# Sparse attention and FFN on one core: first loads reordered, and weight loads tied to the conversion of earlier ones

## The chip, the core and the metric

The kernel runs on one NeuronCore of a Trainium2 chip. The metric is device microseconds of one execution; three runs of the kernel before gave 869.53, 871.46 and 873.02, median 871.46. The engines are TensorE (PE, its weight loads shown as PEld), VectorE (DVE), ScalarE (ACT), GpSimd (POOL) and SyncE (SP), which issues nearly all DMA transfers. Each engine works through its own instructions strictly in the order written.

## The reference

```python
# q, k, v: (8, 8, 576, 64); heads 0-3 local mask, heads 4-7 strided mask, stride 32
scores = where(mask[h], q @ k.T / sqrt(64), -1e9)
attn = softmax(scores);  x = (attn @ v) laid out as (8 * 576, 512)
h = x @ w_in                          # (512, 2048)
out = (h * clip(h + 3, 0, 6) / 6) @ w_out     # (2048, 512)
```

`w_in` and `w_out` arrive as 64-bit floats; each is 8 MB.

## The kernel before

The eight batches are done one after another. For batch 0 attention runs first: four pairs of heads, g = 0 to 3, in the order local, strided, local, strided. For each pair q and k are loaded and turned upright by matmuls with an identity (L372), scores go to PSUM (L609, L601), the softmax runs over DVE, ACT and POOL (L634 to L666), the probabilities are transposed (L685 on DVE for strided pairs, L372 and L721 for local ones), and the product with v is made (L389 for the first local pairs, L736 for strided ones). Two copies (L427 on ACT, L430 on DVE) then make one quarter of x, as a high and a low part. The four quarters x are in the order of the pairs; the products ph (L857 to L859) of the FFN add over all four, so the FFN of batch 0 runs freely only once the fourth quarter is there. Until the first ph there are filler matmuls (L1571, "idle") wherever the plan sees PE unused.

A weight block k (0 to 31; here `parts[k]`, four blocks of w_in, four of w_out, and so on) is 128 x 512 doubles, 512 KB, loaded by one DMA (L274) into `raw`. It is turned into a high and a low single-precision part: `high` (ACT, L282), `low` (ACT, L286), `join` (DVE, L290), `hi` (ACT L304 or POOL L306), `lo` (POOL, L309). Blocks 0 to 7 serve the first four columns of the FFN of batch 0, blocks 8 to 15 the next four.

The order of every engine comes from a planner, `Plan.emit`: each `op` has an engine, an estimated duration, a due time and the keys it reads and writes; the planner simulates, always starting the operation that can start first and, among those, the one that is due first. `early` is the earliest start, `after` the time a load takes in the planner's model of DMA, `room` an extra margin behind an input. What is written out is a fixed order; on the chip the engines keep it, whatever the real times are.

SP issues in this order at the start: q and k of batch 0 (k of g = 0, 1 from ACT), v of g = 0 (L378, L381: rows of 256 bytes), v of g = 1 (L567: 2 KB), weight blocks 0 to 3, v of g = 2 (256 bytes again), v of g = 3, weight blocks 4 to 15, then q, k and v of batch 1 (L358, L567, L362, L367), among which the later weight blocks come.

Of the kernel before, what the change touches and what calls it, by code (L numbers as in the profile page):

```python
# [12 lines left out]
I32 = mybir.dt.int32  # L13
# [6 lines left out]
P = 128  # L20
# [9 lines left out]
TOK = 512  # L30
TURNS = ((0, 2, 1, 3), (2, 0, 3, 1)) + ((0, 2, 1, 3),) * 6
AHEAD = 27.0
OPEN = 6.0
HIENG = {"ACT": 0.63, "POOL": 0.7}

# [25 lines left out]
class Plan:  # L61
# [12 lines left out]
    def op(self, engine, us, fn, reads=(), writes=(), due=0.0, room=0.0, mode="", after=0.0, take=None, give=None, early=0.0):  # L74
        n = len(self.ops)
        before = set()
        for k in reads:
            if k in self.wrote:
                before.add(self.wrote[k])
            self.used.setdefault(k, []).append(n)  # L80
        for k in writes:
            if k in self.wrote:
                before.add(self.wrote[k])
            before.update(self.used.pop(k, ()))
            self.wrote[k] = n
        before.discard(n)
        how = engine if isinstance(engine, dict) else {engine: us}
        self.ops.append((how, fn, before, due, room, mode, after, take, give, early))
        return n
# [85 lines left out]
def attention_ffn(ctx: ExitStack, tc, q, k, v, w_in, w_out, out):  # L175
    nc = tc.nc
# [9 lines left out]
    NQ = 4  # L186
# [3 lines left out]
    wp = ctx.enter_context(tc.tile_pool(name="wp", bufs=1))  # L190
# [7 lines left out]
    op = plan.op  # L198
    tiles = {}

    def new(pool, key, shape, dtype, name):

        tag = "_".join(str(x) for x in key)
        t = tiles[key] = pool.tile(shape, dtype, tag=tag, name=name)
        return t
# [52 lines left out]
    def wkey(w, g, i):  # L258
        return ("w", w, g, i)

    def weight_part(k, w, g, i):
        key = wkey(w, g, i)
        fc = FQ * g if w == "i" else FQ * g + i + 1
        due = T0 + fc * TILE / NFC - 5.0 + 0.01 * k
        fkey = ("x", 1, 1 - (k // 2 % 2 if k < 20 else 0), k % 2)
        name = f"{w}{g}{i}"

        def load():
            if w == "i":
                src = w_in[i * P:(i + 1) * P, g * TOK:(g + 1) * TOK]  # L270
            else:
                src = w_out[(g * FQ + i) * P:(g * FQ + i + 1) * P, :]
            raw = new(wp, key, [P, TOK, 2], I32, f"raw{name}")
            nc.sync.dma_start(raw, src.bitcast(I32).rearrange("p (n t) -> p n t", t=2))  # L274

        def bits():
            raw = tiles[key]
            return raw.rearrange("p n t -> p (n t)")[:, :TOK]

        def high():  # L280
            f = new(xp, fkey, [P, TOK], I32, f"f{name}")
            nc.scalar.activation(f.bitcast(F32), tiles[key][:, :, 1].bitcast(F32), AF.Prelu, scale=2.0 ** -112, alpha=2.0 ** 32)  # L282

        def low():
            raw = tiles[key].bitcast(U16).rearrange("p n (t u) -> p n t u", u=2)[:, :, 0, 1]
            nc.scalar.activation(bits(), raw, AF.Copy, scale=2.0 ** -13, bias=2.0 ** -14 - 0.5)  # L286

        def join():
            f = tiles[fkey]
            nc.vector.scalar_tensor_tensor(out=f, in0=f, scalar=3, in1=bits(),  # L290
                                           op0=ALU.logical_shift_left, op1=ALU.bitwise_or)

        def whole():
            f = tiles[fkey].bitcast(F32)
            return f if w == "i" else f.rearrange("p (h e d) -> p h d e", h=2, d=2)

        def part(x):
            t = tiles[key][:, x]
            return t if w == "i" else t.rearrange("p (h d e) -> p h d e", h=2, d=2)

        def hi(e):
            new(wp, key, [P, 2, TOK], F32R, f"w{name}")
            if e == "ACT":
                nc.scalar.copy(part(0), whole())  # L304
            else:
                nc.gpsimd.tensor_copy(part(0), whole())  # L306

        def lo():
            nc.gpsimd.tensor_tensor(out=part(1), in0=whole(), in1=part(0).bitcast(F32), op=ALU.subtract)  # L309

        op("SP", 0.53, load, writes=[key], due=-49 + 0.01 * k if k < 4 else -48.4 + 0.01 * k if k < 6 else -2 + 0.1 * k if k < 16 else due - 20.0, early=7.0 if k < 16 else due - 30.0, after=1.6 if k < 16 else 1.25)
        op("ACT", 0.68, high, reads=[key], writes=[fkey], due=due - 5, room=LATE + 1.0)
        op("ACT", 0.68, low, writes=[key], due=due - 5)
        op("DVE", 1.05, join, reads=[key], writes=[fkey], due=due - 3)
        op(HIENG, 0, hi, reads=[fkey], writes=[key], due=due - 2)
        op("POOL", 1.3, lo, reads=[fkey, key], writes=[key + ("lo",), key], due=due - 1)


    nn = [0]
# [24 lines left out]
    def timing(g):  # L344
        b = g // NPAIR
        if not b:
            return T0 - 6.0 * (NPAIR - g)
        return wanted[b] - 6.0 - (NPAIR - 1 - g % NPAIR) * (wanted[b] - opens[b]) / NPAIR
# [92 lines left out]
    def pair(g):  # L441
# [3 lines left out]
        loc = h0 < H // 2  # L445
        nm = f"{b}_{c}"
        early = (b == 0) + (g == 0)
        due = timing(g)
# [30 lines left out]
        for x in "qk":  # L479
# [6 lines left out]
            if early:  # L486
# [32 lines left out]
                for h in range(2):  # L519
                    op({"ACT": 0.45, "DVE": 0.4} if loc else {"ACT": 0.65, "DVE": 0.65}, 0, partial(evac, h=h), reads=[tb[h]],  # L520
                       writes=[tkey[x]] if h == 0 else [(tkey[x], 1)], give=tb[h], due=due - 19)
# [13 lines left out]
            op("SP", 3.4 if b > 4 else 2.8, load, writes=[nkey], due=due - 35, early=due - 45, after=2.0)  # L535
            op("DVE", 0.8 if loc else 1.25, tr, reads=[nkey, "plain"], writes=[tkey[x]], due=due - 18, early=max(due - AHEAD, T0 + OPEN), room=LATE)


        first = b == 0 and loc
        vkeys = [("vt",) if loc else ("vs",)]  # L540
        if first:
            vkeys = [wkey("i", NQ - 1, j) if c else ("n", j) for j in range(2)]
# [6 lines left out]
        elif b == 0:  # L549
            vkeys = [wkey("i", NQ - 1, c)]  # L550
# [7 lines left out]
        def load_v():  # L558
# [6 lines left out]
            rows = v[b, h0:h0 + 2].rearrange("j (m a t) d -> a m j (t d)", a=4, t=8)  # L565
            for a in range(4):
                nc.sync.dma_start(tiles[vkey][PAD * a:PAD * a + NPOS].rearrange("p j t d -> p j (t d)"), rows[a])  # L567
        op("SP", 2.6 if first else 1.6 if loc else 2.1, load_v, writes=vkeys, due=(-52, -48.8, -48.7, -48.5)[g] if early else due - 30, early=0 if early else due - 35, after=3.2 if first else 2.0)


        ekeys = [("el" if loc else "es", j) for j in range(2)]
# [4 lines left out]
        w = 2 * PAD if loc else NPOS  # L576
# [37 lines left out]
        for j in range(2):  # L614
# [5 lines left out]
            def keep(j=j):  # L620
# [17 lines left out]
               writes=[ek, st], give=banks[j], due=sd + 0.5)  # L638
# [874 lines left out]
            second_of(s)  # L1513
    nk, no, nz = [0], [0], [0]

    parts = [(w, g, i) for g in range(NQ) for w in "io" for i in range(4)]

    def first_tiles():
        tiles["qplain"] = ap.tile([P, S + STRIDE * PAD], F32, tag="qq", name="qplain")
# [14 lines left out]
    for g in range(NPAIR):  # L1534
        pair(g)
# [4 lines left out]
    for n, part in enumerate(parts):  # L1540
        weight_part(n, *part)
# [3 lines left out]
    for g in range(NPAIR, 4 * NPAIR):  # L1545
        pair(g)
    keep_plain()
    ffn(1)
    for g in range(4 * NPAIR, 5 * NPAIR):
        pair(g)  # L1550
# [54 lines left out]
```

## Time and profile before

| | us |
|---|---|
| median of three runs | 871.46 |
| lowest and highest | 869.53, 873.02 |
| the profiled execution, its own time | 870.54 |
| its span in the profile | 868.8 |

The profile is of one execution, with a mean granted TensorE clock of 0.991. Times in it are microseconds from the start of the span, 1.7 us of the execution lie outside it. A row of the timeline merges like instructions: start, busy time, engine, line, operation, tiles, shape, count, and in brackets the idle time of the engine before it with what ended it. "issue" there means that the engine waited for nothing that the profile shows.

### The profile page before, as it was taken

Reading aid. Unit: us, or ns where it says so; the run is one execution under the profiler, and the core shown is the slowest. Engines: PE = TensorE matmul, PEld = TensorE weight load, DVE = VectorE, ACT = ScalarE, POOL = GpSimd, SP = SyncE. Lnnn points to the kernel's source line nnn. Section 1 sums busy time; section 2 is a strip of 40 time slices with the busy share of each in tenths; the row PEclk is TensorE's granted clock in tenths of the full one; section 3 lists DMA queues with packets and bytes.
Section 4 is the critical chain, followed back from the end, with each engine's and each line's share of the span. In section 5 each row is a group of like instructions: output and inputs, shape, how many; then the busy total and the mean of one; then the engine's idle time right before and its main releaser. Section 6 shows DMA issues by size and latency. Waiting matters only on the chain.

```text
span 868.8 us, 18930 instructions
## 1 busy us (share of the span) xinstructions
PE 846.6 (97%) x6954; PEld 683.0 (79%) x6954; DVE 537.6 (62%) x898; ACT 557.9 (64%) x1246; POOL 615.3 (71%) x606
## 2 busy tenths in 40 slices
PE   8899999999999999999999999999999999999996
PEld 7577778788888788888888888788888778888884
DVE  6588878344454538454546664566767888555586
ACT  4587657678778866877677955776744645454441
POOL 5488876687547799767676994465974987767573
PEclk9899999999999999999999999999999999999998
DMA  8978713798974455899999898876566667866536
GB/s 199 313 158 240 231 30 83 205 290 237 295 216 116 119 129 159 219 268 250 243 285 287 272 314 212 230 206 197 180 203 188 190 179 223 243 195 194 182 122 145
DMA packets 323308, 179.12 MB, mean 206 GB/s; under 512 B 182864, under 2 KB 300368, under 8 KB 323216
## 3 DMA queue, kind: packets, MB, share of 16 engines
q1 hardware_dynamic: 318564, 176.27, 71.8%
q10 hardware_dynamic: 4652, 1.64, 0.9%
q8 instruction: 55, 0.90, 0.4%
q14 instruction: 37, 0.30, 0.1%
HBM read 136.97 MB, written 40.89 MB: 205 GB/s over the span
## 4 chain that ended last, share of the span: by engine, by line
PE 87%; POOL 5%; DVE 4%; ACT 2%; issue 2%; POOLq 0%; DVEq 0%; ACTq 0%
PE P L1130 8%; PE P L1131 8%; PE P L1132 8%; PE cP L1453 5%; PE cP L1454 5%; PE cP L1455 5%; PE acc L834 5%; PE ph L857 5%; PE ph L858 4%; PE ph L859 4%; PE acc L835 4%; PE acc L836 4%; PE acc L1215 4%; PE acc L1217 3%; PE acc L1216 3%; PE pv L736 2%
## 5 line engine op out<-in xcount | busy, mean ns | idle before, releaser
L1471 DVE SCALAR_TENSOR_TENSOR C<-cP,C 128x512 f32<-128x512 f32 x96 | 65.7, 687 | 40.5 <-PE cP L1455 39.8
L795 POOL TENSOR_TENSOR gl<-u,gh 128x512 fp32r<-128x512 f32 x48 | 65.2, 1360 | 34.1 <-ACT gh L791 17.9
L1142 DVE TENSOR_TENSOR G<-P,G 128x512 f32<-128x512 f32 x64 | 44.0, 689 | 65.1 <-PE P L1132 52.7
L1130 PE MATMUL P<-B_T,wr 128*128 128x512 f32 x192 | 76.1, 397 | 3.9 <-ACT G L1137 2.3
L834 PE MATMUL acc<-wo,gh 128*128 128x512 f32 x192 | 77.3, 403 | 0.0
L836 PE MATMUL acc<-wo,gl 128*128 128x512 f32 x192 | 75.2, 392 | 0.3 <-POOL gl L795 0.2
L835 PE MATMUL acc<-wo,gh 128*128 128x512 f32 x192 | 75.1, 391 | 0.0
L1131 PE MATMUL P<-B_T,wr 128*128 128x512 f32 x192 | 74.9, 390 | 0.0
L1132 PE MATMUL P<-B_T,wr 128*128 128x512 f32 x192 | 74.9, 390 | 0.0
L1137 ACT COPY G<-P 128x512 f32<-128x512 f32 x64 | 37.5, 586 | 52.3 <-PE P L1132 51.9
L1368 POOL TENSOR_TENSOR sp<-G,sp 128x512 fp32r<-128x512 f32 x34 | 47.5, 1408 | 24.8 <-ACT sp L1364 22.6
L666 POOL TENSOR_TENSOR e<-e,st 128x144 f32<-128x144 f32 (+1 forms) x64 | 44.2, 693 | 18.8 <-DVE st L662 15.7
L780 DVE SCALAR_TENSOR_TENSOR u<-u,ph 128x512 f32<-128x512 f32 x48 | 32.8, 684 | 38.2 <-ACT u L777 38.1
L857 PE MATMUL ph<-x,wi 128*128 128x512 f32 x128 | 52.6, 411 | 2.3 <-ACT x L427 1.2
L701 ACT COPY atloc<-e 32x192 f32<-32x192 f32 x144 | 50.8, 353 | 2.5 <-DVE e L691 1.1
L858 PE MATMUL ph<-x,wi 128*128 128x512 f32 x128 | 51.0, 398 | 0.6 <-DVE x L430 0.5
L859 PE MATMUL ph<-x,wi 128*128 128x512 f32 x128 | 50.8, 397 | 0.0
L777 ACT ACTIVATE u<-ph,three 128x512 f32<-128x512 f32 x48 | 33.0, 687 | 27.2 <-PE ph L859 26.9
L1130 PE MATMUL P<-B_B,wr 128*128 128x512 f32 x120 | 47.1, 393 | 0.0
L1131 PE MATMUL P<-B_B,wr 128*128 128x512 f32 x120 | 46.8, 390 | 0.0
L1130 PEld LDWEIGHTS P<-B_T,wr 128*128 128x128 f32 x192 | 36.1, 188 | 13.7 <-ACT G L1137 3.6
L1132 PE MATMUL P<-B_B,wr 128*128 128x512 f32 x120 | 46.8, 390 | 0.0
(604 smaller groups left out, 2648.1 us busy)
## 6 DMA issues: line engine op xcount, KB each, us to landing
wr<-dA SPq DMA_DIRECT2D x72, 256.0 KB
or<-do SPq DMA_DIRECT2D x32, 512.0 KB
wr<-dSu SPq DMA_DIRECT2D x48, 256.0 KB
wr<-dSv SPq DMA_DIRECT2D x48, 256.0 KB
or<-do SPq DMA_DIRECT2D x48, 256.0 KB
rawi<-in_moe_w_in_dram SPq DMA_DIRECT2D x16, 512.0 KB
rawo<-in_moe_w_out_dram SPq DMA_DIRECT2D x16, 512.0 KB
do<-wo SPq DMA_DIRECT2D x16, 512.0 KB
```

The costliest lines, as they stand in the source:

```text
L701: nc.scalar.copy(at[PAD * (a + h):PAD * (a + h) + PAD, :, rows], e[rows, :, PAD * h:PAD * h + PAD])
L795: (nc.vector if tail else nc.gpsimd).tensor_tensor(out=to, in0=src(), in1=tiles[gk[0]].bitcast(F32), op=ALU.subtract)
L834: nc.tensor.matmul(acc, gh, woh, start=fc == 0, stop=False)
L835: nc.tensor.matmul(acc, gh, wol, start=False, stop=False)
L836: nc.tensor.matmul(acc, gl, woh, start=False, stop=end)
L857: nc.tensor.matmul(ph, wih, xh, start=n_ == 0, stop=False)
L858: nc.tensor.matmul(ph, wih, xl, start=False, stop=False)
L859: nc.tensor.matmul(ph, wil, xh, start=False, stop=n_ == NCC - 1)
L1130: nc.tensor.matmul(ph, wh, xh, start=fresh and k == 0, stop=False, skip_group_check=not fresh)
L1131: nc.tensor.matmul(ph, wh, xl, start=False, stop=False, skip_group_check=not fresh)
L1132: nc.tensor.matmul(ph, wl, xh, start=False, stop=k == 1, skip_group_check=not fresh)
L1471: nc.vector.scalar_tensor_tensor(out=tiles[ck], in0=tiles[bank], scalar=1.0 / 6.0, in1=tiles[ck], op0=ALU.mult, op1=ALU.add)
```

## The change

Three things change. The due times of the first loads are altered so that SP's order becomes: v of g = 0, v of g = 1, weight blocks 0 and 1, v of g = 2, weight blocks 2 and 3, v of g = 3, block 4. After `lo` of block k, for k from 0 to 10, POOL writes one element pair into the tile `raw` of block k + 5; that tile is made then. The load of block k + 5 writes the same tile, so for blocks 5 to 15 SP waits for that write, and the planner knows the load to depend on `lo` of the block five ahead. Sizes, arithmetic and the blocks from 16 on are as before.

```diff
+PACE = 5
...
+    parts = [(w, g, i) for g in range(NQ) for w in "io" for i in range(4)]
+    raws = {}
+
+    def raw_of(k):
+        if k not in raws:
+            raws[k] = new(wp, wkey(*parts[k]), [P, TOK, 2], I32, "raw{}{}{}".format(*parts[k]))
+        return raws[k]
+
     def weight_part(k, w, g, i):
         key = wkey(w, g, i)
+        paced = PACE <= k < 16
...
-            raw = new(wp, key, [P, TOK, 2], I32, f"raw{name}")
+            raw = raw_of(k)
...
         def lo():
             nc.gpsimd.tensor_tensor(out=part(1), in0=whole(), in1=part(0).bitcast(F32), op=ALU.subtract)
-
-        op("SP", 0.53, load, writes=[key], due=-49 + 0.01 * k if k < 4 else -48.4 + 0.01 * k if k < 6 else -2 + 0.1 * k if k < 16 else due - 20.0, early=7.0 if k < 16 else due - 30.0, after=1.6 if k < 16 else 1.25)
+            if k + PACE < 16:
+                nc.gpsimd.memset(raw_of(k + PACE)[:1, :1], 0)
+
+        op("SP", 0.53, load, reads=[("paced", k)] if paced else [], writes=[key], due=(-49, -48.99, -48.8, -48.79)[k] if k < 4 else -48.4 + 0.01 * k if k < 6 else -2 + 0.1 * k if k < 16 else due - 20.0, early=7.0 if k < 16 else due - 30.0, after=1.6 if k < 16 else 1.25)
...
-        op("POOL", 1.3, lo, reads=[fkey, key], writes=[key + ("lo",), key], due=due - 1)
+        op("POOL", 1.3, lo, reads=[fkey, key], writes=[key + ("lo",), key] + [("paced", k + PACE)] * (k + PACE < 16), due=due - 1)
...
-        op("SP", 2.6 if first else 1.6 if loc else 2.1, load_v, writes=vkeys, due=(-52, -48.8, -48.7, -48.5)[g] if early else due - 30, early=0 if early else due - 35, after=3.2 if first else 2.0)
+        op("SP", 2.6 if first else 1.6 if loc else 2.1, load_v, writes=vkeys, due=(-52, -49.5, -48.9, -48.7)[g] if early else due - 30, early=0 if early else due - 35, after=3.2 if first else 2.0)
```

## Rows read from the trace of the kernel before

**Rows 1.** From the page: busy time of each engine with its instructions, and the DMA queue that carries code.

```profile
PE 846.6 (97%) x6954; PEld 683.0 (79%) x6954; DVE 537.6 (62%) x898; ACT 557.9 (64%) x1246; POOL 615.3 (71%) x606
q8 instruction: 55, 0.90, 0.4%
```

**Rows 2.** Stretches of the span: start and end, length, busy time and instruction count of each engine, granted clock, DMA share, GB/s.

```profile
0.00:23.62 23.62, 21.45 (x602) 16.94 (x603) 15.74 (x42) 11.31 (x26) 11.28 (x34) 1.00 0.84 208
...
20.00:30.00 10.00, 4.95 (x162) 4.07 (x160) 6.83 (x21) 4.29 (x10) 2.94 (x6) 0.86 0.81 224
30.00:40.00 10.00, 10.00 (x125) 6.43 (x124) 5.43 (x13) 6.68 (x20) 6.81 (x10) 0.80 0.97 358
40.00:50.00 10.00, 9.93 (x135) 7.45 (x135) 7.37 (x18) 8.90 (x20) 6.70 (x9) 1.00 1.07 322
50.00:60.00 10.00, 8.32 (x41) 6.19 (x38) 7.50 (x11) 8.36 (x17) 9.25 (x8) 0.83 0.50 94
60.00:70.00 10.00, 9.93 (x166) 7.83 (x165) 8.07 (x16) 8.05 (x16) 9.84 (x10) 1.00 0.87 224
145.00:243.00 98.00, 98.00 (x979) 78.79 (x979) 45.71 (x96) 76.08 (x211) 63.44 (x78) 1.00 0.84 244
```

**Rows 3.** The timeline of PE, 20 to 39 us.

```profile
22.73 0.89 PE L389 MATMUL pv<-at,v 64*64 64x32 f32 x44
27.93 1.07 PE L389 MATMUL pv<-at,v 64*64 64x32 f32 x28 [4.31 <-issue]
28.93 4.21 PE L1571 MATMUL idle<-ident 128*128 128x384 f32 x6
33.07 1.63 PE L736 MATMUL pv<-atstr,v 128*64 128x72 f32 x32
34.62 1.14 PE L601 MATMUL ps<-kt,qt 64*64 64x36 f32 x64
35.69 2.20 PE L1571 MATMUL idle<-ident 128*128 128x384 f32 x6
38.69 0.50 PE L857 MATMUL ph<-x,wi 128*128 128x512 f32 x1
```

**Rows 4.** DMA packets of three stretches: 17.9 to 21.0, 21.0 to 25.2, and 25.2 to 25.4 with the code queue in it. A weight row is one packet of 4 KB, so the packets under 8 KB less those under 2 KB are weights.

```profile
DMA packets 217, 0.82 MB, mean 266 GB/s; under 512 B 16, under 2 KB 16, under 8 KB 217
...
DMA packets 822, 1.26 MB, mean 299 GB/s; under 512 B 545, under 2 KB 545, under 8 KB 822
...
DMA packets 153, 0.07 MB, mean 327 GB/s; under 512 B 149, under 2 KB 149, under 8 KB 152
...
q8 instruction: 1, 0.02, 41.5%
```

**Rows 5.** The same view of 13 to 16 us, when v of g = 0 is coming in.

```profile
DMA packets 1566, 0.46 MB, mean 154 GB/s; under 512 B 1523, under 2 KB 1523, under 8 KB 1566
```

**Rows 6.** The timeline of SP's queue: start and length of the issue of each group of loads.

```profile
16.40 2.79 SPq L274 DMA_DIRECT2D rawi<-in_moe_w_in_dram  x4
19.23 0.66 SPq L378 DMA_DIRECT2D v<-in_v_dram  x1
23.25 1.86 SPq L381 DMA_DIRECT2D v<-in_v_dram  x2
29.15 2.37 SPq L274 DMA_DIRECT2D rawo<-in_moe_w_out_dram  x4
34.41 4.01 SPq L274 DMA_DIRECT2D rawo<-in_moe_w_out_dram  x4
39.46 7.65 SPq L358 DMA_DIRECT2D qn<-in_q_dram  x4
59.39 1.95 SPq L358 DMA_DIRECT2D qn<-in_q_dram  x4
61.44 2.07 SPq L358 DMA_DIRECT2D kn<-in_k_dram  x4
63.55 2.73 SPq L274 DMA_DIRECT2D rawi<-in_moe_w_in_dram  x4
```

**Rows 7.** Timelines of DVE, ACT and POOL, 25 to 38 us.

```profile
25.59 1.75 DVE L685 STREAM_TRANSPOSE atstr<-e 32x256 f32<-32x256 f32 x4
29.29 0.46 DVE L430 TENSOR_TENSOR x<-pv,x 128x288 fp32r<-128x288 f32 x1 [1.95 <-ACT x L427]
30.87 0.82 POOL L649 TENSOR_TENSOR e<-e,st 96x384 f32<-96x384 f32 x1 [4.86 <-DVE st L645]
33.55 1.28 POOL L309 TENSOR_TENSOR wi<-fi,wi 128x512 fp32r<-128x512 f32 x1
37.01 0.55 POOL L641 TENSOR_TENSOR e<-e,mtri 128x144 f32<-128x144 f32 x1 [2.18 <-ACT e L627]
```

**Rows 8.** Timelines of DVE and PE, 48 to 58 us.

```profile
48.90 2.37 DVE L290 SCALAR_TENSOR_TENSOR fo<-fo,rawo 128x512 int32<-128x512 int32 x3
51.20 0.61 DVE L430 TENSOR_TENSOR x<-pv,x 128x256 fp32r<-128x256 f32 x1
51.78 1.20 DVE L290 SCALAR_TENSOR_TENSOR fi<-fi,rawi 128x512 int32<-128x512 int32 x1
49.27 1.22 PE L736 MATMUL pv<-atstr,v 128*64 128x72 f32 x32
53.57 0.50 PE L858 MATMUL ph<-x,wi 128*128 128x512 f32 x1 [0.48 <-DVE x L430]
```

**Rows 9.** The shortest memset of POOL, from the timeline of the first microseconds.

```profile
0.24 0.10 POOL L1589 MEMSET const-float32-0.0<- 128x1 f32 x1 [0.24 <-issue]
```

**Rows 10.** Timelines of POOL and PE, 55 to 67 us: `lo` of weight block 8, and the first product of the second group of columns, which reads it.

```profile
55.98 1.28 POOL L309 TENSOR_TENSOR wi<-fi,wi 128x512 fp32r<-128x512 f32 x1
66.05 0.39 PE L857 MATMUL ph<-x,wi 128*128 128x512 f32 x1
```

## What the change is expected to do

> **What bounds the kernel now.** I read the page first: PE is busy 846.6 us of the 868.8 [rows 1]. In the stretches PE is full from 60 us on, at full clock, with DVE and POOL well below it in the bulk; what it lacks lies before 60 us: 5 of 10 us busy in 20 to 30, and a clock of 0.86, 0.80 and 0.83 in three of the four stretches after 20 [rows 2]. So the change, which acts before 70 us, is worth what it moves the moment from which the FFN runs freely. That is 53.57, when the fourth quarter of x arrives [rows 8].
>
> The next view is PE's timeline there [rows 3]. In the middle of one product, after 44 of 72 like instructions, PE stops for 4.31 us, from 23.62 to 27.93, and the trace names nothing that it waits for. All its inputs are there: the same tiles serve the instructions before and after. I read this as a wait for code. The code queue moved 55 blocks in the whole run, 0.90 MB, so 16 KB each, and PE has 2 x 6954 = 13908 instructions [rows 1], 253 to a block; none of the other engines has near as many. PE had run 602 + 603 of them when it stopped [rows 2]. One block starts between 25.2 and 25.4 [rows 4], 2.6 us before PE goes on.
>
> Why so late? The four weight loads were issued from 16.40 to 19.2 [rows 6]. Their 4 x 128 rows are 512 packets of 4 KB; 201 ran from 17.9 to 21.0, 277 from 21.0 to 25.2, and only 3 in the stretch in which the code block starts [rows 4]. The block began just when the weights had drained. Its request must have come before the stop, since 1205 instructions had then been run and the pieces of code come one by one; about 21 us is my estimate.
>
> [...]
>
> **The change, part by part.**
>
> *Order of v and weights.* Blocks 0 and 1, then v of g = 2, then blocks 2 and 3. Nothing changes up to block 1, so PE reaches the stop at 23.62 as before. Of 256 weight packets, 201 are gone by 21.0 [rows 4]; at 277 in 4.2 us, 66 a us, the rest takes 0.8, until 21.8. Behind them come the 256-byte rows of v: 2 x 64 x (8 + 9) + 64 = 2240. Those of g = 0 ran at 1523 in 3 us, 508 a us [rows 5], so they take 4.4 us. If the code block has to wait only for the weights it starts at 21.8, and PE resumes 2.6 later, at 24.4, which is 3.5 earlier. If it waits for all of v as well it starts at 26.2: no gain. SP needed from 19.23 to 25.1 to hand out these v loads [rows 6], so at 21.8 about a third is not yet in the queue, and I take a start at 22.8 and a return at 25.4: 2.5 earlier, bounds 0 and 3.5.
>
> [...]
>
> *The clock.* With a shorter stop the clock may hold. Fillers 2.0 us, the product at 33.07 against its like at 49.27 0.4 (1.63 and 1.22), and the rest of the stopped product 0.5 (28 in 1.07 against 44 in 0.89): 2.9 us at most, 0 at least [rows 3, 8]. Near the nearer row: 51 to 53.6, a wait of some 2 us, is also followed by a lower clock, 0.83 in 50 to 60 [rows 2]; so I take half, 1.4.
>
> *What the others allow.* DVE transposes until 27.34 and would take the next copy then, 1.95 before 29.29; the product at 33.07 needs these transposes, so it could start at about 27.5, 5.6 earlier [rows 3, 7]. POOL is idle 4.86 before 30.87 and 2.18 before 37.01 [rows 7]. With DVE 1.95 ahead, its chain up to the end of `lo` of block 0 comes 1.95 to 2.3 earlier, at about 32.5 instead of 34.83, and the mask operation follows at once: 37.01 less 32.6 is 4.4. So stop and clock together, 2.5 + 1.4 = 3.9, stay under the 4.4 that POOL allows. I take 3.9; bounds 0 and 4.4.
>
> *Blocks 2 and 3 later, v of g = 2 earlier.* Each passes the other in SP's queue, 3.0 us or so by rows 6; q, k and the other v keep their places. Block 2 then has all packets in by about 28.5 to 30 and its `lo` ran as one of two from 40.15 on; block 3 later still. Their conversion hides this. Nothing waits for the earlier v. If the cover were gone, 3 us would come back.
>
> *Pacing.* It adds 11 memsets on POOL, bound by the shortest in the trace, 0.10 [rows 9], and by 0.2 with the hand-over: before the fourth quarter of x there are about 4 of them on POOL's way, 0.4 to 0.8; POOL is 6.7 to 9.3 of 10 busy there [rows 2], so I take 0.3 lost and 0 to 0.8 as bounds. The loads 5 to 15, now issued in one stream from 29 to 38.4 [rows 6], go out one by one after `lo` of the block five ahead. Behind them on SP stand q, k and v of batch 1, for which DVE's transposes of batch 1 wait; the next pair's q follows at 59.39, once such a transpose has emptied its tile [rows 6], so the first is wanted only shortly before, and with the stream gone these loads can pass ahead of block 5. The code blocks requested at 30 to 47 find fewer weights ahead, but PE showed no stop there, so nothing is gained.
>
> The later loads push conversions of blocks 6 to 8 back, out of the way of the fourth quarter: three joins end at 51.27 and hold up the copy at 51.20, and the join of 1.20 at 51.78 holds up the last copy at 52.90 [rows 8]. Without them I see 0.5 + 0.3 = 0.8 us; as others may move there, I take 0.5, bounds 0 and 0.8.
>
> Sum: 3.9 + 0.5 - 0.3 = 4.1 us, bounds -0.8 and 5.2. The profiled execution took 870.54, 868.8 in its span, so it would take 866.4; that execution lies 0.9 below the median of 871.46, which would become 867.4. Between the two I say 866.9.
>
> **The rivals.**
>
> *The stop stays.* Either the block waits for v instead of the weights, or the stop is no wait for code. Speaking for it: at 25.2 to 25.4 149 small packets ran beside 3 weight ones [rows 4], so v was no bar to the block, but nor is it shown that the weights were. Time: 4.1 less 3.9, so 871.3, or one stop later, when blocks 2 and 3 meet the next code block at 25 to 28, the same. [...]
>
> *More than that.* The clock holds fully and x comes without the joins: 4.4 + 0.8, and the half clock after 53.57, which shows in the 0.83 of 50 to 60 [rows 2], that is 10 x 0.17 = 1.7, may go too. 6.9 less 0.3: 864.
>
> *Slower: block 8 comes too late.* Its `lo` ended at 57.26 and the product that reads it ran at 66.05 [rows 10]: 8.8 us in hand. After the change SP may have q and k of the next pair ahead of it, which were issued at 59.39 and 61.44 only after a transpose on DVE [rows 6]. 4.1 earlier, they end at 59.4; block 8 is issued then, 1.5 us to the first packets (16.40 to 17.9), some 4 us through its five conversion steps: 65, against a need at 62. PE stops 3 us, at up to 2.9 for the clock, and block 13, tied to `lo` of 8, repeats it: up to 12 in all less 4.1, so 874 to 879, say 876. It decides from the point at which SP has block 8 behind that pair. Against it: the planner knows the tie and gives each load 3 us of margin.
>
> **How the numbers follow.** The forecast, 866.9 with its own range 864.8 to 869.6, has 0.46. The stop stays, 869.8 to 873.2: 0.25. More, 861.5 to 864.8: 0.15. Slower, 873 to 879: 0.14. 0.5%, 4.4 us, is about what a measurement here can tell: the bounds are 867.1 and 875.8. Faster: 0.15 and just over six in ten of the forecast's 0.46, 0.44. Slower: most of the last, 0.11, and 0.01 from strays, 0.12. The same: 0.44. The range 862.6 to 873.5 leaves out about 2 in 10.
>
> **What would show it.** In the changed profile: the stop on line L389 falls to about 2 us and the code block starts near 22.8; six fillers after it in some 3 us; the first ph near 35 rather than 38.69; the fourth quarter used near 49.5 rather than 53.57; PE full after it. Wrong, if the stop keeps its 4.3 us or a new "issue" stop of over 1 us stands at 30 to 33; if PE waits on POOL's `lo` between 58 and 75; or if ph comes earlier and the end does not.

## The result: slower by half a per cent

The kernel after the change takes 875.45 us (median of 18 runs, 870.95 to 878.85) against 871.16 for the kernel before (18 runs, 865.19 to 873.89). The ratio is 1.0056, with a 95% interval of 1.0038 to 1.0073: slower by 4.3 us, where the sum of the forecast had made it 4.1 us faster, and outside the range. Single executions of memsets_only (942 and 2933 us) and first_tied (2409 us) ran in another state and are left out of their medians and ratios. The profiled execution of the kernel after took 873.07, 871.3 of it in its span, 2.4 below the median.

From the page of the kernel after, the two lines that answer to [rows 1]. PE is busy 1.8 us longer, the span is 2.5 us longer, and the code queue moves the same 55 blocks.

```profile
PE 848.4 (97%) x6956; PEld 684.6 (79%) x6956; DVE 535.5 (61%) x896; ACT 555.9 (64%) x1241; POOL 619.0 (71%) x624
q8 instruction: 55, 0.90, 0.4%
```

Stretches of the kernel after, with the columns of [rows 2].

```profile
20.00:30.00 10.00, 9.53 (x203) 7.90 (x204) 6.65 (x21) 4.50 (x13) 3.73 (x7) 0.58 0.91 240
30.00:40.00 10.00, 10.00 (x139) 6.80 (x139) 7.65 (x17) 7.22 (x22) 7.38 (x11) 1.00 0.71 140
40.00:50.00 10.00, 8.45 (x98) 6.04 (x94) 8.93 (x19) 6.26 (x13) 8.21 (x14) 0.83 0.53 169
50.00:60.00 10.00, 9.19 (x186) 6.77 (x186) 7.53 (x11) 8.70 (x17) 8.92 (x12) 1.00 0.76 211
60.00:70.00 10.00, 9.45 (x41) 7.13 (x40) 8.54 (x20) 6.69 (x13) 9.92 (x12) 1.00 0.97 223
```

In 20 to 30 us PE is now busy 9.53 of 10 instead of 4.95, but at a granted clock of 0.58: at 0.50 until 28.3, for 4.2 / 0.5 = 8.4 us of it. In 40 to 50 us, where the kernel before was full at full clock, it lacks 1.5 us of work and the clock is 0.83.

PE's timeline in the kernel after, to be held against [rows 3].

```profile
14.66 0.48 PE L613 MATMUL ps<-kplain,qplain 64*64 64x36 f32 x17
17.10 0.90 PE L613 MATMUL ps<-kplain,qplain 64*64 64x36 f32 x47 [1.96 <-issue]
27.35 1.33 PE L401 MATMUL pv<-at,v 64*64 64x32 f32 x44
29.15 0.66 PE L401 MATMUL pv<-at,v 64*64 64x32 f32 x28 [0.47 <-issue]
29.74 2.20 PE L1582 MATMUL idle<-ident 128*128 128x384 f32 x6
31.87 1.22 PE L748 MATMUL pv<-atstr,v 128*64 128x72 f32 x32
37.54 0.69 PE L869 MATMUL ph<-x,wi 128*128 128x512 f32 x1
43.94 0.50 PE L869 MATMUL ph<-x,wi 128*128 128x512 f32 x1 [0.92 <-POOL wi L316]
45.29 0.69 PE L871 MATMUL ph<-x,wi 128*128 128x512 f32 x1 [0.63 <-POOL rawo L321]
54.57 0.50 PE L870 MATMUL ph<-x,wi 128*128 128x512 f32 x1 [0.24 <-DVE x L442]
```

The stop of 4.31 us after 44 of 72 products with v is down to 0.47, and what follows runs at full clock (1.00 from 28.4 to 37.5), as forecast. But a stop of 1.96 us stands at 15.14, where this execution of the kernel before had none, and the half clock that follows it (0.50 from 18.2 to 28.3) lasts to about 28 us. So the first ph comes at 37.54 instead of 38.69: 1.15 earlier, not 3.9. Then PE waits twice for POOL, at 43 and 45 us, and the fourth quarter of x is used at 54.57 instead of 53.57 [rows 8].

### The profile page after: what moved, and what is told of

Read it like the earlier page. It is cut to its first block, busy times and chain, and to the rows that moved or that the text cites. A ratio compares the mean times of both kernels' runs of the same rounds, so it can differ in the third digit from the quotient of the medians.

```text
span 871.3 us, 18974 instructions
## 1 busy us (share of the span) xinstructions
PE 848.4 (97%) x6956; PEld 684.6 (79%) x6956; DVE 535.5 (61%) x896; ACT 555.9 (64%) x1241; POOL 619.0 (71%) x624
## 3 DMA queue, kind: packets, MB, share of 16 engines
q1 hardware_dynamic: 318564, 176.27, 72.2%
## 4 chain that ended last, share of the span: by engine, by line
PE 84%; POOL 6%; DVE 3%; DMA 3%; issue 2%; ACT 1%; SPq 0%; ACTq 0%; POOLq 0%; DVEq 0%
PE P L1142 8%; PE P L1144 8%; PE P L1143 8%; PE cP L1465 5%; PE cP L1466 5%; PE cP L1467 5%; PE acc L846 5%; PE ph L869 4%; PE acc L848 4%; PE acc L847 4%; PE ph L871 4%; PE ph L870 4%; PE acc L1227 4%; PE acc L1229 3%; PE acc L1228 3%; PE pv L412 2%
## 5 line engine op out<-in xcount | busy, mean ns | idle before, releaser
L807 POOL TENSOR_TENSOR gl<-u,gh 128x512 fp32r<-128x512 f32 x48 | 64.5, 1345 | 33.8 <-ACT gh L803 25.9
L792 DVE SCALAR_TENSOR_TENSOR u<-u,ph 128x512 f32<-128x512 f32 x48 | 32.7, 684 | 45.4 <-ACT u L789 45.3
L848 PEld LDWEIGHTS acc<-wo,gl 128*128 128x128 f32 x192 | 36.0, 188 | 12.9 <-POOL gl L807 5.3
```

The source lines that it names most:

```text
L807: (nc.vector if tail else nc.gpsimd).tensor_tensor(out=to, in0=src(), in1=tiles[gk[0]].bitcast(F32), op=ALU.subtract)
L848: nc.tensor.matmul(acc, gl, woh, start=False, stop=end)
```

## The experiments

All ratios are to the kernel before, run on the same chip between the runs of the kernel named.

| kernel | order of the engines | ratio | 95% interval |
|---|---|---|---|
| after | new plan, 11 loads wait | 1.0056 | 1.0038 to 1.0073 |
| order_only | a third plan, no load waits | 1.0078 | 1.0047 to 1.0108 |
| pacing_only | a fourth plan, 11 loads wait | 1.0067 | 1.0041 to 1.0094 |
| belief | a fifth, nothing else changed | 1.0089 | 1.0073 to 1.0106 |
| belief_2 | a sixth, nothing else changed | 1.0055 | 1.0030 to 1.0080 |
| swap_alone | of before, but SP | 1.0020 | 0.9999 to 1.0040 |
| weights_last | of before, but SP | 0.9993 | 0.9980 to 1.0006 |
| ties_kept | of before, but SP; 11 loads wait | 1.0026 | 1.0005 to 1.0048 |
| change_kept | of before, but SP; 11 loads wait | 1.0034 | 1.0016 to 1.0052 |
| fewer_warm | of before, fewer fillers | 1.0018 | 0.9994 to 1.0042 |
| no_memset | of after, no load waits | 1.0020 | 0.9994 to 1.0045 |
| elsewhere_unmoved | of after, no load waits | 1.0016 | 0.9992 to 1.0041 |
| first_tied | of after, 5 loads wait | 1.0038 | 1.0014 to 1.0061 |
| last_tied | of after, 6 loads wait | 1.0031 | 1.0009 to 1.0053 |
| memsets_unmoved | of before, memsets | 1.0011 | 0.9992 to 1.0029 |
| memsets_only | of before, memsets, tiles moved | 1.0052 | 1.0026 to 1.0078 |
| shift_only | of before, tiles moved | 1.0033 | 1.0009 to 1.0056 |
| memset_elsewhere | of after, memsets, tiles moved | 1.0094 | 1.0069 to 1.0119 |

### Each part by itself, as the planner writes it

**order_only**: the new due times, no pacing.

```diff
-PACE = 5
+PACE = 16
```

> Only the new order of the first loads (v of g = 2 between weight blocks 1 and 2); no load is tied to a conversion and there are no memsets. Theory P, the pacing costs the time and the order is worth what the prediction gave it: faster than before by 2 to 4 us, about 868. Theory O, the order itself costs it, because the waits of TensorE for code only move to other places before 30 us: 2 to 4 us slower than before, about 874. The profile tells them apart by the start of the first ph (38.69 before) and by what comes after it.

Measured: 877.28 us. **pacing_only**: the pacing, with the old due times.

```diff
-due=(-49, -48.99, -48.8, -48.79)[k] if k < 4
+due=-49 + 0.01 * k if k < 4
-due=(-52, -49.5, -48.9, -48.7)[g]
+due=(-52, -48.8, -48.7, -48.5)[g]
```

> The old order of the first loads, with blocks 5 to 15 paced by the conversion five ahead and the memsets. Theory P: about 4 us slower than before, 875, with waits of TensorE on GpSimd between 40 and 100 us. Theory O: within 1.5 us of before, 871.

Measured: 877.60. Each part alone costs no less than both together, so neither kernel tells what its part does to the chip: each edit lets the planner write the whole order anew.

### What a new plan costs when nothing on the chip is changed

**belief** and **belief_2** change one number each that only the planner reads: the time that a load is taken to need, and the time from which its model of DMA is free.

```diff
-after=1.6 if k < 16
+after=1.7 if k < 16
```

```diff
-FIRST = 3.4
+FIRST = 3.5
```

> The kernel before with one number of the planner changed: it believes that each of weight blocks 0 to 15 takes 1.7 instead of 1.6 us. No load, wait or instruction is added; the planner only writes another order (about as many lines of each engine move as under the change). If what the change lost is mostly the loss of a plan that happened to fit, this loses 2 to 6 us too, 873 to 877. If the change's own loads and waits cost the time, this stays within 1.5 us of 871.

> The kernel before with another number of the planner changed: it believes the first transfer to end at 3.5 instead of 3.4 us. Nothing is added or taken away. If plans near that of before are worse in general, 873 to 878 again, as belief with 877.3; if belief was one bad draw, 868 to 872.

Measured: 877.29 and 874.91. A tenth of a microsecond in a belief, with every load, size and wait of the program as before, costs 4 to 8 us. The waits of PE in belief between 430 and 560 us, where the kernel before waits 0.7 us in all (columns: us in total, times, longest):

```profile
PE acc L1217 <- POOL gl_7c L795: 1.6, 1, 1.6
PE P L1131 <- POOL B_B L1064: 1.2, 1, 1.2
PE P L1130 <- DVE G L780: 0.5, 1, 0.5
```

PE waits there, 400 us behind the loads whose number was changed, for operations of POOL and DVE, whose order is new too. So a change that goes through this planner can't be priced by its own operations alone.

**before_again** is the kernel before, for a second profile.

> The kernel before, unchanged, for a second profile. If the stops of TensorE for code vary from one execution to the next, the stop is here at another count (449, 705 or 961 instead of 1217, each 256 apart) or of another length, and the first ph is 1 us or more away from 38.69. If they belong to the program, all is as before: one stop, at 1217, of 4 to 5 us.

Measured: 870.75. Its PE timeline, the stops without a named wait:

```profile
11.48 0.83 PE L609 MATMUL ps<-kplain,qplain 64*32 64x64 f32 x60 [0.55 <-issue]
17.75 0.90 PE L601 MATMUL ps<-kplain,qplain 64*64 64x36 f32 x47 [1.92 <-issue]
29.77 1.04 PE L389 MATMUL pv<-at,v 64*64 64x32 f32 x28 [1.91 <-issue]
36.81 0.30 PE L601 MATMUL ps<-kt,qt 64*64 64x36 f32 x3 [0.43 <-issue]
```

One program, two executions: a single stop of 4.31 us [rows 3] in the one, four of 0.55, 1.92, 1.91 and 0.43 in the other, with the same time at the end. The first ph is at 40.04 here, 1.35 later than in the execution on which the forecast was built.

### Is the stop a wait for code?

**fewer_warm** takes 16 filler products off the start, so that every later instruction of PE stands nearer to the beginning of the code, and changes no wait.

```diff
-FEW = 46
+FEW = 30
```

> The kernel before with 30 instead of 46 small warming matmuls at the start: 16 fewer, 64 rows of TensorE in the trace. If the stop at 23.62 us is a wait for a block of code, it stands at the same count of instructions, 602 + 603, and so 64 rows later in the program: the 28 rows of pv on line 389 run on without a break, and the stop shows at the end of the fillers or at the product of line 736. If it is a wait for data, it stays in the middle of line 389. Time: 0 to 4 us less than before, as the stop then falls in a place where fillers stand anyway.

Measured: 873.63, ratio 1.0018: not 0 to 4 us faster, but within the scatter of the kernel before. The stops in its PE timeline:

```profile
14.64 0.85 PE L609 MATMUL ps<-kplain,qplain 64*32 64x64 f32 x28 [3.22 <-issue]
37.54 0.81 PE L1571 MATMUL idle<-ident 128*128 128x384 f32 x2 [1.53 <-issue]
```

Counted in PE's records, weight loads, matmuls and the few waits between them, the stops of the other kernels fall at 449, 705, 961 or 1217, in weights_last and before_again also at 1473, which lie 256 apart; the 4.31 is the one at 1217 (1205 in the prediction, without 12 waits). Here the program is 64 records shorter ahead of them, and they stand again at 449 and 1217, which are now other instructions: 28 from the end of a group of scores, and among the fillers of line 1571. The products with v run through. So the stop belongs to a place in the code, 256 instructions apart, 16 KB by [rows 1], and not to what the instruction computes. That part of the forecast held. The 20 profiles have 44 such stops of over 0.25 us in the first 45 us, and in each of them PE goes on 2.3 to 3.2 us after the first packet of a code block.

### The parts in the order of the kernel before

Here the planner's order is kept on PE, ACT, DVE and POOL, and only SP's queue is rewritten behind it. **swap_alone** lets v of g = 2 and blocks 2 and 3 change places; **weights_last** puts v of g = 3 ahead of the two blocks too.

```diff
+new_at = [self.tags["v2"], self.tags["w2"], self.tags["w3"]]     # swap_alone
+new_at = [self.tags[x] for x in ("v2", "v3", "w2", "w3")]        # weights_last
```

> The kernel before with its whole plan kept, every engine's order as it was, but v of g = 2 exchanged with weight blocks 2 and 3 in SyncE's queue: the new order of the first loads without what the planner makes of it. If the loads themselves cost the time of order_only (6 us): 875 to 878. If that time comes from the order that the planner then writes for all engines: 868 to 872, the same as before or 1 to 3 us faster as the prediction had it.

> The kernel before with its whole plan kept, but SyncE's queue reads: blocks 0 and 1, v of g = 2, v of g = 3, blocks 2 and 3. If the code blocks wait behind the 4 KB rows of weights, the block for count 1217 is requested while only v is ahead of it and the stop there is 1.5 us or less, against 4.5, 2.1 and 3.2 in before, before_again and swap_alone; the first ph then comes 0.5 to 3 us earlier than in these and the time is 867 to 870. If code waits behind any traffic, the stop stays at 2 to 4 us and the time is 870 to 873.

Measured: 872.28 and 870.68. The swap brings nothing and costs at most little. The stop at 1217 is 2.97 us long in swap_alone, although v of g = 2 goes ahead of blocks 2 and 3 there; weights_last has none at 1217 and one of 0.87 at 1473, and its time is that of the kernel before all the same. **change_kept** adds the pacing to swap_alone: each of the loads 5 to 15 stands right behind the `lo` that frees it, and waits for its memset. **ties_kept** has the pacing without the swap.

```diff
+late = {tags[f"lo{k}"]: tags[f"w{k + 5}"] for k in range(11)}
+seq = [y for x in seq if x[2] not in late.values()
+       for y in ([x, (x[0], x[1], late[x[2]], "SP")] if x[2] in late else [x])]
```

> Both parts of the change, the new order of the first loads and blocks 5 to 15 tied by memsets to the conversion five ahead, but with the order of the kernel before on TensorE, VectorE, ScalarE and GpSimd (memsets added); in SyncE's queue each tied load stands right behind the conversion that frees it. If the loss of the changed kernel lies in the order that the planner wrote, this is within 2 us of before, 869 to 873. If it lies in the loads, the waits and the memsets, it is 875 or more.

> The kernel before with the pacing alone and every engine's order kept, but for SP, where the load of each of the blocks 5 to 15 stands right behind the point at which lo of the block five ahead frees it; v and the first four blocks stay in their old order. Theory W, the wait of the loads is what costs: 2.5 to 4.5 us over the kernel before, as change_kept (ratio 1.0034), most of it before 60 us. Theory O, it is the wait only together with the order of the plan of the kernel after, or chance: within 1.5 us.

Measured: 873.95 and 872.45. With the swap or without it, the waiting of the loads costs 2 to 3 us in an order that is not made for it. Waits of ties_kept, SP between 20 and 80 us and PE between 36 and 60:

```profile
SPq L288 <- POOL rawi L325: 10.1, 4, 4.1
SPq L288 <- POOL rawo L325: 7.9, 6, 4.6
...
PE ph L873 <- ACT x L443: 2.0, 1, 2.0
PE ph L874 <- DVE x L446: 0.3, 1, 0.3
```

SP stands 18 us for memsets, and PE waits 2.3 us for the fourth quarter of x, 1.7 in the kernel before. In its profile the first ph is 1.3 later than in the kernel before and the last product 3.1.

### The memsets, and a tile that moved the others

**no_memset** is the kernel after without the memsets: its plan, and no load that waits. **memset_elsewhere** lets POOL write a spare tile instead, so that the memsets are there and no load waits. **memsets_only** has these memsets in the kernel before.

```diff
-            if k + PACE < 16:
-                nc.gpsimd.memset(raw_of(k + PACE)[:1, :1], 0)       # no_memset
```

```diff
+    spare_raw = const.tile([1, 1, 2], I32, name="spare_raw")
...
-                nc.gpsimd.memset(raw_of(k + PACE)[:1, :1], 0)
+                nc.gpsimd.memset(spare_raw[:1, :1], 0)              # memset_elsewhere
```

> The changed kernel with its planned order, but without the memsets, so that SyncE does not wait for a conversion before it issues blocks 5 to 15; the order in every queue stays that of the changed kernel. If the wait on the chip and the memsets cost the time (theory P, first form): back to 869 to 872. If it is the order that the planner writes once it believes the loads to come late (theory P, second form), or the order of the first loads (theory O): as the changed kernel, 874 to 876.

> The changed kernel with its planned order and its eleven memsets, but these write a spare tile, so SyncE waits for no conversion. Between no_memset (872.3) and the changed kernel (875.5): if GpSimd's memsets cost, about 875; if SyncE's wait costs, about 872.

> The kernel before with nothing changed but 11 short memsets: POOL writes one element pair into a spare tile behind lo of blocks 0 to 10. Every engine keeps its order, the loads are not tied to anything, and the spare tile is read by nobody. It measures the disputed cost by itself. Theory A, the memsets cost time of their own wherever they stand (memset_elsewhere less no_memset was 5.6 us with one order): 4 to 6 us over the kernel before, and PE's timeline shows waits on POOL at 40 to 60 us. Theory B, they cost only their 0.1 us each and the hand-over, and the 5.6 came from the order that they met there: within 1.5 us of the kernel before (their bound in the prediction was 0 to 0.8). The stop at the instruction counts 449, 705, 961 or 1217 may fall anywhere in this one profile, 0.7 to 4.5 us long, and is no evidence for either.

Measured: 872.25, 877.87 and 875.28. The memsets seemed to cost 5 us wherever they stood. But the profile of memsets_only has no wait on a memset, and its products with v go on at 30.79, 2.9 later than in [rows 3], before the first memset runs at 37.61. Something else was different: the spare tile lies among the constants, and in the built program 738 of the 746 places in SBUF are 32 bytes further on. So the tile without memsets (**shift_only**), and the memsets with the tile at the end of SBUF, where it moves nothing (**memsets_unmoved**, and **elsewhere_unmoved** in the plan of the kernel after):

```diff
+    spare_raw = const.tile([1, 1, 2], I32, name="spare_raw")        # shift_only, nothing else
```

```diff
+    zp = ctx.enter_context(tc.tile_pool(name="zp", bufs=1))
+    spare_raw = zp.tile([1, 1, 2], I32, name="spare_raw")           # the other two
```

> The kernel before, instruction for instruction, with an unused tile of 8 bytes among the constants, which moves the tiles behind it by 32 bytes in SBUF. Theory A (the memsets cost the 4.5 us of memsets_only): the time of the kernel before, within 1.5 us. Theory C (the place of the tiles costs it): 3.5 to 5.5 us over it. Theory D (neither; the loss is in when the stops for code and the loads from scratch fall, and any change redraws that): anything from -1 to 5.

> The kernel before with the same 11 memsets as memsets_only, but into a tile at the end of SBUF, so that no other tile moves. Theory A: 3.5 to 5.5 us over the kernel before. Theory C: within 1.5 us of it. Theory D: -1 to 5, with no relation to shift_only.

> The plan of the kernel after with the 11 memsets into that tile at the end of SBUF: memset_elsewhere (877.87) without the moved tiles. Theory A: as memset_elsewhere, 5 to 6 us over no_memset (872.25), so 877 to 878.5. Theory C: within 1.5 us of no_memset, so 871 to 874, which would leave the 3.2 us between the kernel after (875.45) and no_memset to the loads that wait for the memsets.

Measured: 873.11, 871.01 and 870.41. With no tile moved the memsets cost nothing that can be measured, and a tile that nobody reads costs 2 to 3 us; with memsets the moved tiles cost 4 us in the order of the kernel before (1.0052 against 1.0011) and 7 in that of the kernel after (1.0094 against 1.0016). The main DMA queue on the page of memsets_unmoved (packets, MB, share of 16 engines' span):

```profile
q1 hardware_dynamic: 318564, 176.27, 71.4%
```

and of shift_only:

```profile
q1 hardware_dynamic: 318564, 176.27, 73.1%
```

The same packets and bytes take 1.7 points more of the DMA engines' time; the pages of memsets_only and memset_elsewhere show 73.2 and 73.9%, those of before and after 71.8 and 72.2, and none without a moved tile is above 72.4. Packets of 256 bytes take 20.4 ns on average in shift_only against 19.3 in the kernel before and 18.9 in the kernel after, those of 512 bytes 29.8 against 28.6 in both. What in the new places makes them slower is not shown, nor where PE pays for it. In the profile of shift_only, which took 878.35, the longest of its 12 runs, PE waits between 430 and 580 us:

```profile
PE acc L1216 <- DMA or<-do: 2.8, 3, 1.5
PE P L1131 <- ACT G L1138: 1.6, 2, 1.0
PE P L1131 <- DMA wr<-dSu: 1.0, 1, 1.0
```

The wait for the load `or` is absent in the kernel before and 0.4 in before_again, but also 1.2 to 1.6 in swap_alone, fewer_warm and memsets_unmoved, where no tile was moved.

### Which of the waiting loads

**first_tied** lets only blocks 5 to 9 wait in the plan of the kernel after, **last_tied** only blocks 10 to 15; the other memsets go to the tile at the end of SBUF.

```diff
-                nc.gpsimd.memset(raw_of(k + PACE)[:1, :1], 0)
+                nc.gpsimd.memset((raw_of(k + PACE) if k < 5 else spare_raw)[:1, :1], 0)    # last_tied: k >= 5
```

> The kernel after, but only the loads of blocks 5 to 9 wait for a memset; the six other memsets go to a tile at the end of SBUF. Theory W with the cost at the first blocks, whose conversions the first products need: as the kernel after, ratio 1.004 to 1.007. If the cost is at the later blocks: as elsewhere_unmoved, 1.000 to 1.003.

> The kernel after, but only the loads of blocks 10 to 15 wait for a memset; the five other memsets go to a tile at the end of SBUF. The mirror of first_tied: 1.000 to 1.003 if the cost is at the first blocks, 1.004 to 1.007 if at the later ones. If both this and first_tied are at 1.000 to 1.003, the wait costs only as a whole, or the 3 to 5 us between the kernel after and elsewhere_unmoved aren't due to it.

Measured: 873.77 and 874.06. Both lie between the two values expected: in one and the same order, the ratio grows from 1.0016 and 1.0020 with no waiting load over 1.0031 and 1.0038 with six and five to 1.0056 with eleven. Neighbours in this row overlap in their intervals, its ends hardly do.

## Why the prediction was wrong

**What held.** The stop is a wait for code (fewer_warm). q and k of batch 1 passed ahead of block 5, at 29.80. The rival on the slower side did not come about: `lo` of block 8 ended at 64.26 and the product that reads it, the first ph of the second group, ran at 68.52, with no wait for it; that 875.45 lies in that rival's range is chance.

**The step that failed first: 3.9 for the stop and the clock.** It took one execution's stop for the kernel's, and the weights ahead of the code block for the cause of its length. Of the 20 profiles, 18 stop at 705 for 1.1 to 2.5 us; the one on which the forecast was built is one of the two that do not, and it has the longest stop of all at 1217. There the ten profiles with v of g = 2 ahead of blocks 2 and 3 stop for 1.3 us on average (0 to 3.00), the ten with the old order of these loads for 1.3 too (0 to 4.31). So the 0.47 of the kernel after is no effect of the order that these runs can show. Nor does a code block have to wait until the weights have drained. Packets of the kernel after from 26.3 to 27.3 and from 13.4 to 14.4:

```profile
DMA packets 106, 0.40 MB, mean 403 GB/s; under 512 B 10, under 2 KB 10, under 8 KB 105
...
q8 instruction: 1, 0.02, 5.8%
...
DMA packets 627, 0.17 MB, mean 170 GB/s; under 512 B 626, under 2 KB 626, under 8 KB 626
...
q8 instruction: 1, 0.02, 8.7%
```

The first of these blocks starts at 26.83 among 95 weight rows in one microsecond. The second starts at 13.92, before the first weight load is issued at 15.52, and yet PE stands still until 17.10: the same code queue let PE run dry 512 instructions earlier than in [rows 3], ahead of all loads that the change moves, and the half clock behind it (0.50 from 18.2 to 28.3) held for 10 us. That the block for the stop at 23.62 was asked for at about 21 was the author's estimate, and no view shows a request; it starts at 25.28, 1.66 after the stop, where the two blocks of the kernel after start 1.22 and 1.85 ahead of theirs (at 15.14 and 28.68). Over the profiles in which no tile was moved, the first ph stood at 37.54, 38.85, 41.74, 40.21 and 37.20 with the order of the kernel after (after, no_memset, elsewhere_unmoved, first_tied, last_tied), mean 39.1, and at 38.69, 40.04, 40.24 and 39.98 with that of the kernel before (before, before_again, memsets_unmoved, ties_kept), mean 39.7; swap_alone, weights_last and change_kept, with the new order of these loads and the rest as before, had 40.15, 38.41 and 38.27. The term is worth some 0.6 us, within the scatter, not 3.9.

**A step that failed too: "Their conversion hides this", costed at nothing.** The forecast shifted the old order and kept it; the change wrote a new one. POOL's timeline in the kernel after:

```profile
41.80 1.22 POOL L678 TENSOR_TENSOR e<-e,st 128x144 f32<-128x144 f32 x2
43.13 0.20 POOL L1549 MEMSET vloc<- 32x128 f32 x1
43.28 0.60 POOL L316 CAST wi<-fi 128x512 fp32r<-128x512 f32 x1
43.96 1.28 POOL L319 TENSOR_TENSOR wi<-fi,wi 128x512 fp32r<-128x512 f32 x1
45.18 0.09 POOL L321 MEMSET rawo<- 1x2 int32 x1
```

The high part of block 2 is made at 43.28, behind softmax work of the next pair, and its `lo` ends at 45.24; in the kernel before ACT shared in the high parts of blocks 1 and 2 (POOL at 38.70, ACT at 39.67), and `lo` of block 2 was the second of two that ended at 42.67. PE waits 0.92 for the one and 0.63 for the other, and the clock halves at about 45.4 (0.50 from 45.5 to 48.8). The load is not what is late: ACT takes up block 2 at 37.87 straight behind other work, without idle time. Waits of PE up to 60 us in elsewhere_unmoved, where no load waits for anything, show the same pair:

```profile
PE ph L871 <- POOL wi L318: 0.9, 1, 0.9
PE ph L873 <- POOL spare_raw L323: 0.6, 1, 0.6
```

Between the first ph and 47 us of the kernel before, the five profiles with the new order lose 3.7, 2.1, 3.6, 3.4 and 3.6 us against it, before_again, memsets_unmoved and ties_kept nothing. swap_alone, with the same late blocks in the old order, loses nothing there: it is the order, not the loads. The size is about that of the 3 us which the prediction named "if the cover were gone". But this loss is made up by 60 us, because PE then waits less for the fourth quarter (0.5 us instead of 1.7 in after) and the half clock that follows it in the kernel before (0.50 from 54.5 to 57.8) is missing (1.00 from 54 to 58). The two stretches in the kernel before, then in the kernel after, with the columns of [rows 2]:

```profile
0.00:60.00 60.00, 51.76 (x924) 38.71 (x925) 40.31 (x94) 36.96 (x84) 35.28 (x61) 0.91 0.83 231
60.00:100.00 40.00, 39.41 (x407) 30.75 (x406) 34.33 (x64) 29.22 (x54) 36.14 (x32) 1.00 0.78 217
...
0.00:60.00 60.00, 53.30 (x1048) 40.76 (x1049) 42.05 (x94) 34.19 (x78) 37.19 (x71) 0.89 0.77 195
60.00:100.00 40.00, 36.85 (x250) 28.29 (x249) 30.61 (x60) 27.49 (x51) 34.75 (x34) 1.00 0.96 268
```

Idle time and lower clock up to 60 us add up to 8.2 + 5.4 = 13.6 in the kernel before and 6.7 + 6.6 = 13.3 in the kernel after; from 60 to 100 they are 0.6 and 3.2. Over the five profiles with the new order the mean is 14.2 up to 60 us, over before, before_again, memsets_unmoved and ties_kept it is 14.6; from 60 to 150 it is 4.7 against 1.6. What the new order costs for good lies there: between 60 and 150 us PE waits 2.4 to 3.1 us for POOL's `gl` (L807 in after) in all five profiles with it, and 0.2 to 0.6 in those four. By the ratios of no_memset and elsewhere_unmoved the order costs 1.4 to 1.7 us over the whole, with intervals that hold 1, so that the waits are shown but not that they cost the whole kernel anything.

**A step that was mis-sized: pacing, costed at 0.3.** The memsets themselves are worth that or less (memsets_unmoved). The waiting of the loads, for which the forecast put nothing, is not: 3.2 us between no_memset and the kernel after, 2 to 3 in ties_kept and change_kept. SP's waits between 20 and 80 us of the kernel after:

```profile
SPq L284 <- POOL rawo L321: 9.7, 5, 3.5
SPq L284 <- POOL rawi L321: 8.3, 4, 3.0
```

No single wait of PE makes up the 3 us. The clock does: as an estimate, a run loses by it its span times what its mean granted clock lacks to 1. On average that is 11.0 us over the 18 runs of the kernel after, 10.0 and 9.2 in first_tied and last_tied, and 7.2 and 8.1 in no_memset and elsewhere_unmoved, where no load waits; the kernel before has 7.3 to 7.7 beside these (standard errors 0.3 to 1.5). The rest of the span is 862.3 in the kernel after, 863.7 and 862.1 in no_memset and elsewhere_unmoved, about 861 in the kernel before. So of the 4.3 us lost some 3.5 are time at the lower clock, of which the forecast had counted on 1.4 us less. In the order of the kernel before it is otherwise: ties_kept and change_kept lose 0.4 and 1.4 by the clock and 1.9 and 1.4 in the rest.

The gain of 0.5 from joins that go out of the way of the fourth quarter failed with it: the quarter is used 1.0 later, not earlier.

**What stays open.** When, and after what, the clock is lower in the runs that have no profile is not shown. Nor is it shown what makes a code block come in time in one execution and 2 us late in the next.

## What to carry to other kernels

A planner that writes the whole order anew is part of every edit: first measure what a meaningless edit costs (here 4 to 8 us for 0.1 us in a belief), and test an edit in the old order, rewritten by hand, before its own effect is judged. A stop seen in one profile is one draw; take a second profile of the same kernel before pricing its removal. And look where the tiles lie after an edit: one of 8 bytes among the constants moved 738 of 746 places by 32 bytes, cost 2 to 3 us, and looked like a cost of the instructions that wrote it.

## What the runs showed of the hardware

PE stops for code at places 256 instructions apart, 0.3 to 4.3 us long, up to four of them in the first 40 us (before_again), and goes on 2.3 to 3.2 us after the block's first packet; after a stop of 1.96 us in the kernel after the granted clock was 0.55 from 17.1 to 27.1.
